# Channel layer: splits and sums on VectorE alone, token sums kept in DRAM, both first products of part one's last groups issued together

## The chip, the cores and the metric

The kernel runs on one core of a Trainium2 chip. The metric is device time in microseconds (us), the median of three runs. TensorE (PE in the profile) multiplies, VectorE (DVE), ScalarE (ACT) and GpSimd (POOL) do the elementwise work, and SyncE (SP) issues the DMAs.

## The reference

Three layers follow each other on 4 sequences of 576 tokens with 512 channels: windowed attention, a low-rank token mix with a channel layer, and a gated spatial layer. The change sits in the channel layer, the two lines with `w_ch1` and `w_ch2`.

```python
x = attention(q, k, v)                          # 8 heads, window of 128, bias by distance
h = x.transpose(0, 2, 1) @ U @ V
u = x + h.transpose(0, 2, 1)
ch = np.maximum(u @ w_ch1, 0.0) @ w_ch2         # 512 -> 2048 -> 512
y = u + ch
h = np.maximum(y @ w_in, 0.0)                   # then gate, spatial mix, w_out
...
```

## The kernel before

Every float32 operand of a large product is split into a high part (rounded to a narrower format on ScalarE) and a low part (operand minus high part, `minus`, L563). A product is then three matmuls: high by high, low weight by high, high weight by low.

The channel layer's 2048 hidden channels are worked off in four parts of 512. **Part 0** uses plain products: six early groups of 256 tokens run beside attention, and two last groups of 384 tokens follow it (`ffn_group`). A group has a first product (`u @ w_ch1`, L513 to L515, 48 matmuls in a group of 384) and a second product (L550 to L552, again 48). **Parts 1 to 3** each have three groups of 768 tokens (`seven_group`), named a, r and c, in the orders a r c, c a r, r a c. A group's first product is done for pairs of blocks with seven products instead of eight (L705 to L707, 84 matmuls), for which sums and differences of blocks of the weights (`pair_forms`) and of the tokens (`token_forms`) are made and split first. Its second product has 96 matmuls. The seven forms are named "11", "2", "1", "3", "12", "22" and "4"; three of them ("11", "12", "4") are plain blocks of u, the other four are sums. A token form holds two k-blocks, each with a high and a low tile of 128 x 384.

When a part starts, its weights are new: w_ch1 blocks are loaded, decoded from their 64-bit form by four VectorE instructions of 512 columns (L416, L417, L420, L423; tile `st`), turned into forms (256 columns each), and the four w_ch2 blocks (`w2s`) are loaded, decoded, rounded on ScalarE (L370) and given their low part on L568 (VectorE) or L569 (GpSimd). The low part of the last w_ch2 block of a part is what the first second-product matmuls of that part's first group need last. After each first product VectorE combines the PSUM results (tile `c`, L712) and takes the low part of the hidden values (tile `hl`, L719); after each second product it adds PSUM into `y` (L750).

Which engine takes a split or a sum is chosen by a planner (`Plan.run`). It lists all tasks with an engine or several, a cost, a priority and their dependencies, and lays them out in time; each engine then executes its list strictly in order. For `ANY = ("POOL", "DVE")` (L572) it takes whichever engine can start. In the plan, an instruction on GpSimd and one on VectorE that both work in SBUF do not overlap (`port=True`); on the chip nothing keeps them apart. Loads go through SyncE's queue, also in the order of the plan. Token forms are single-buffered: 20 slots `xd` and 8 slots `x` hold exactly one set of seven.

Of the kernel before, what the change touches and what calls it, by code (L numbers as in the profile page):

```python
# [74 lines left out]
def f32(ap):  # L75
    return ap.bitcast(F32)
# [31 lines left out]
class Ring:  # L108
# [3 lines left out]
    last = {}  # L112
# [164 lines left out]
def mm(n, m=128):  # L277
    return (max(n, 2 * m) + m / 4) / 2400


def dve(n):
    return n / 960 + 0.066
# [6 lines left out]
def act(n, src=0.06, aps=0):  # L289
    return n / 1200 + src + 0.09 * aps  # L290
# [7 lines left out]
def tile_kernel(ctx, tc, qT, kT, v, U, V, w1, w2, w_in, wspT, bsp, w_out, bias, out):  # L298
# [42 lines left out]
    def in_psum():  # L341
        return psum

    r_wa = Ring(in_left, "wa", 0, more=[f"wa_{i % 12}" for i in range(8, 20)])
    r_w1, r_w2 = (Ring(in_left, "wa", 0, more=[f"wa_{i + j}" for j in range(4)]) for i in (0, 4))
# [149 lines left out]

    def ffn_group(t0, n, wts, prio, first, evac, early):

        hs, ls = split_u(t0, n, evac, early)
        nf = len(wts)
        hid = []  # L500
        for i in range(0, nf, 2 if early else 1):
            per = min(2, nf - i) if early else 1
            if not early:
                turn[0] += 1
            f1 = (r_f1 if early or turn[0] % 4 == 0 else r_at).new([128, per, n], F32)
            for j in range(per):
                wt = wts[i + j][0]

                def f1mm(f1=f1, j=j, wt=wt):
                    for k in range(4):  # L510
                        (a, ia, _), (l, il, _) = hs[k], ls[k]
                        o = f1[:, j]
                        nc.tensor.matmul(o, wt[:, 0, k], a[ia], start=k == 0, stop=False)  # L513
                        nc.tensor.matmul(o, wt[:, 1, k], a[ia], start=False, stop=False)
                        nc.tensor.matmul(o, wt[:, 0, k], l[il], start=False, stop=k == 3)  # L515

                P.add("PE", 12 * mm(n), f1mm, r=[p for x in hs + ls for p in x[2]] + [wt.part(0), wt.part(1)],
                      w=[f1], prio=prio)
            hh, hl = r_h.new([128, per, n], F32R), r_h.new([128, per, n], F32R)
            P.add("ACT", act(per * n), lambda f1=f1, hh=hh: nc.scalar.activation(  # L520
                out=hh.ap(), in_=f1.ap(), func=AF.Relu), r=[f1], w=[hh], prio=evac)
            P.add("DVE", dve(per * n), lambda f1=f1, hh=hh, hl=hl: nc.vector.scalar_tensor_tensor(
                out=hl.ap(), in0=f1.ap(), scalar=0.0, in1=f32(hh.ap()), op0=ALU.max, op1=ALU.subtract),
                r=[f1, hh], w=[hl], prio=evac)
            hid += [(hh, hl, j) for j in range(per)]

            if not early:
                if i == 0:
                    accs = [r.new([128, 1, n], F32) for r in (r_acc, r_sc, r_sc, r_sc)]
                for e in range(4):  # L530
                    second(wts, hid, i, (e,), accs[e], n, prio)
        if early:
            for e in (0, 2):
                acc = r_acc.new([128, 2, n], F32)
                for i in range(nf):
                    second(wts, hid, i, (e, e + 1), acc, n, prio)
                collect(t0, n, (e, e + 1), acc, first, evac)
        else:
            for e in range(4):
                collect(t0, n, (e,), accs[e], first, evac)  # L540

# [29 lines left out]

    ANY = ("POOL", "DVE")  # L572
    FORMS = ("11", "2", "1", "3", "12", "22", "4")
# [55 lines left out]

    def token_forms(which, prio):  # L630

# [9 lines left out]
        for k in range(2):  # L641
# [26 lines left out]
            def plain(name, to=None):  # L668
                hi, lo = res[to or name][k]
                kb, ts = (k, t1) if name == "11" else (k + 2, t1 if name == "12" else t2)  # L670
                for b, s, m, o in ts:
# [4 lines left out]
                          lambda m=m, o=o: f32(hi[:, o : o + m]), r=[ub, hi.part(o)], w=[lo.part(o)], prio=prio)  # L676

            plain("11")
            total("3", (k + 2, 1), (k, 1))
# [7 lines left out]
            split("4", "22")  # L687
            plain("22", "4")
        return res

# [317 lines left out]
    for g in range(NB):  # L1008
        ffn_group(g * 256, 256, parts_w[0], 1e4 + g, True, K["evac"], True)

# [4 lines left out]

    base = 2e4
    for t0 in range(NB * 256, NT, N3):
        ffn_group(t0, N3, parts_w[0], base, True, base - 0.5, False)
        base += 1
    xf, last = None, None  # L1020
    for qi, order in ((1, "arc"), (2, "car"), (3, "rac")):
        forms = [pair_forms(qi, pair, base - K["pf"][pair]) for pair in range(2)]
        w2s = []
        for f in range(4):
            r0 = (sum(PARTS[:qi]) + f) * 128
            w2s.append((None, weights(r_wa, block(w2, r0, r0 + 128, 0, E), 1, E, base - K["p2"] + f / 10, ways=ANY)))
        for which in order:
            if which != last:
                xf, last = token_forms(which, base - K["xf"]), which
            seven_group(which, xf, forms, w2s, base, base - 0.5)  # L1030
            base += 1
# [229 lines left out]

K = dict(parts=(4, 4, 4, 4), flex='xeht', cp=0, wp=0, low=6, w0=7, w0s=0.6, nb=6, evac=40.0, nst=3, d0=7, d0s=0.91, lowd=5, nq=3, pn=1, pf=(1.6, 1.4), p2=1.2, xf=0.7, pi=(1.3, 0.9))

# [39 lines left out]
```

## Time and profile before

| | |
|---|---|
| median of 3 runs | 744.98 us (744.17 to 745.14) |
| the profiled execution | 746.02 us |
| its span, first to last instruction | 744.2 us |
| TensorE busy | 717.3 us, 96% of the span |
| VectorE busy | 535.0 us, 72% |
| ScalarE busy | 339.1 us, 46% |
| GpSimd busy | 189.0 us, 25% |
| mean granted TensorE clock | 0.995 |

The time of an execution is its span and what lies around it (1.8 us here). TensorE's busy share is a modelled one: matmuls are pipelined, and each starts about 0.175 us after the one before (384 columns) while it is shown 0.34 us long. So TensorE is read from the starts and from its idle time, not from busy time. Attention fills about the first 196 us, the last two groups of part 0 the time to 238 us, parts 1 to 3 the time to 531 us, the spatial layer the rest.

### The profile page before, as it was taken

The numbers are of one execution on the slowest core, as the hardware profiler recorded it, in microseconds if no ns is written. First come the engines' busy times: TensorE is split into PE (matmuls) and PEld (weight loads), VectorE is DVE, ScalarE is ACT, GpSimd is POOL, SyncE is SP. The second block draws the span as 40 slices with busy tenths as digits, with TensorE's granted clock in tenths as the row PEclk, the third lists the DMA queues.
The fourth block names the chain that finished last, engine by engine and source line by source line (L and its number), as shares of the span: only waits on it lengthen the run. The fifth ranks groups of instructions, "written<-read, shape, count | busy, mean of one in ns | idle before, by whom it ended". The sixth has DMA issues, their size and how long they took to land.

```text
span 744.2 us, 14920 instructions
## 1 busy us (share of the span) xinstructions
PE 717.3 (96%) x5808; PEld 670.0 (90%) x5808; DVE 535.0 (72%) x1403; ACT 339.1 (46%) x920; POOL 189.0 (25%) x232
## 2 busy tenths in 40 slices
PE   7877999999999999999999998999999999999998
PEld 5656988888999999999999998999999899898896
DVE  5989978685648999598995989978989426326141
ACT  5777757373414724246152462524564333333322
POOL 1243330210622425123231323421335101002000
PEclk9999999999999999999999999999999999999999
DMA  7765313100006000212001230006320100100102
GB/s 226 251 212 145 107 49 99 49 19 2 1 1 196 4 1 1 78 42 108 1 1 29 85 114 1 1 0 199 104 74 1 43 15 1 58 15 1 57 1 71
DMA packets 29164, 45.83 MB, mean 62 GB/s; under 512 B 5029, under 2 KB 18341, under 8 KB 29093
## 3 DMA queue, kind: packets, MB, share of 16 engines
q1 hardware_dynamic: 29092, 44.87, 18.9%
q8 instruction: 46, 0.75, 0.5%
q14 instruction: 26, 0.20, 0.1%
HBM read 39.85 MB, written 4.72 MB: 60 GB/s over the span
## 4 chain that ended last, share of the span: by engine, by line
PE 78%; DVE 13%; issue 4%; DMA 3%; ACT 1%; SPq 1%; POOL 1%; ACTq 0%; POOLq 0%; DVEq 0%
PE sc L552 7%; PE sc L551 7%; PE sc L550 6%; PE at L705 5%; PE at L707 5%; PE at L706 5%; PE sc L1088 3%; PE sc L1090 3%; PE sc L1089 3%; PE at L1090 2%; PE at L1088 2%; PE at L1089 2%; DVE hl L719 2%; PE at L880 2%; PE at L918 2%
## 5 line engine op out<-in xcount | busy, mean ns | idle before, releaser
L551 PE MATMUL sc<-h,wa 128*128 128x384 f32 x312 | 105.6, 339 | 4.5 <-DVE wa L568 4.5
L550 PE MATMUL sc<-h,wa 128*128 128x384 f32 x312 | 105.4, 338 | 0.2 <-ACT wa L370 0.2
L552 PE MATMUL sc<-hl,wa 128*128 128x384 f32 x288 | 98.6, 342 | 0.6 <-DVE hl L719 0.5
L569 POOL TENSOR_TENSOR wa<-st,wa 128x512 fp32r<-128x512 f32 (+2 forms) x44 | 45.9, 1050 | 178.0 <-ACT wa L370 142.7
L850 ACT ACTIVATE p<-p,nmax 128x192 f32<-128x192 f32 (+1 forms) x144 | 61.5, 431 | 10.1 <-DVE nmax L845 10.0
L551 PEld LDWEIGHTS sc<-h,wa 128*128 128x128 f32 x312 | 59.0, 189 | 5.4 <-DVE wa L568 5.4
L712 DVE TENSOR_TENSOR c<-at,c 128x384 f32<-128x384 f32 x90 | 49.7, 552 | 16.5 <-PE at L707 15.8
L705 PE MATMUL at<-xd,wa 128*128 128x384 f32 x180 | 60.9, 338 | 0.0
L706 PE MATMUL at<-xd,wa 128*128 128x384 f32 x180 | 60.8, 338 | 0.0
L707 PE MATMUL at<-xd,wa 128*128 128x384 f32 x180 | 60.8, 338 | 0.0
L550 PEld LDWEIGHTS sc<-h,wa 128*128 128x128 f32 x312 | 59.0, 189 | 0.5 <-ACT wa L370 0.5
L552 PEld LDWEIGHTS sc<-hl,wa 128*128 128x128 f32 x288 | 54.5, 189 | 1.2 <-DVE hl L719 1.2
L750 DVE TENSOR_TENSOR y<-sc,y 128x384 f32<-128x384 f32 (+1 forms) x96 | 40.8, 449 | 15.9 <-PE sc L552 15.6
L370 ACT CAST wa<-st 128x256 fp32r<-128x256 f32 (+1 forms) x70 | 32.6, 491 | 42.6 <-DVE st L423 28.6
L845 DVE CUSTOM_DVE_ANT_0 p<-sc,bias 128x192 f32<-128x192 f32 (+1 forms) x144 | 40.0, 327 | 9.3 <-PE sc L834 9.2
L834 PE MATMUL sc<-kr,qr 64*64 64x192 f32 (+2 forms) x576 | 33.7, 334 | 9.1 <-DMA kr<-in_kT 4.4
L719 DVE SCALAR_TENSOR_TENSOR hl<-c,h 128x384 fp32r<-128x384 f32 x54 | 37.5, 708 | 0.4
L568 DVE TENSOR_TENSOR u<-y,u 128x576 fp32r<-128x576 f32 x9 | 6.6, 753 | 41.8 <-ACT u L1101 41.8
L834 PEld LDWEIGHTS sc<-kr,qr 64*64 64x64 f32 x576 | 22.3, 141 | 14.9 <-issue 5.1
L717 ACT ACTIVATE h<-c 128x384 fp32r<-128x384 f32 x54 | 28.3, 524 | 14.1 <-DVE c L712 13.5
L705 PEld LDWEIGHTS at<-xd,wa 128*128 128x128 f32 x180 | 33.8, 188 | 0.1
L706 PEld LDWEIGHTS at<-xd,wa 128*128 128x128 f32 x180 | 33.8, 188 | 0.0
(350 smaller groups left out, 2154.3 us busy)
## 6 DMA issues: line engine op xcount, KB each, us to landing
wa<-in_w SPq DMA_DIRECT2D x32, 512.0 KB, 4.5
qr<-in_qT SPq DMA_DIRECT2D x16, 288.0 KB, 3.8
kr<-in_kT SPq DMA_DIRECT2D x16, 288.0 KB, 4.2
vr<-in_v SPq DMA_DIRECT2D x16, 256.0 KB, 2.9
wa<-in_w_in SPq DMA_DIRECT2D x8, 512.0 KB, 4.5
out<-h SPq DMA_DIRECT2D x15, 256.0 KB, 2.0
wb<-in_w_out SPq DMA_DIRECT2D x4, 512.0 KB, 4.6
raw<-in_wspT SPq DMA_DIRECT2D x4, 288.0 KB, 2.8
```

Source lines behind the costliest of these rows:

```text
L550: nc.tensor.matmul(o, wt[:, 0, 0, c], hh[:, j], start=i == 0 and x == 0, stop=False, skip_group_check=True)
L551: nc.tensor.matmul(o, wt[:, 1, 0, c], hh[:, j], start=False, stop=False, skip_group_check=True)
L552: nc.tensor.matmul(o, wt[:, 0, 0, c], hl[:, j], start=False, stop=i == len(wts) - 1, skip_group_check=True)
L569: "POOL": (pool_tt(n), lambda: nc.gpsimd.tensor_tensor(out=out(), in0=in0(), in1=in1(), op=op)),
L705: nc.tensor.matmul(o.ap(), wh()[:, k], xh.ap(), start=start and k == 0, stop=False, skip_group_check=True)
L706: nc.tensor.matmul(o.ap(), wl()[:, k], xh.ap(), start=False, stop=False, skip_group_check=True)
L707: nc.tensor.matmul(o.ap(), wh()[:, k], xl.ap(), start=False, stop=k == 1, skip_group_check=True)
L712: P.add("DVE", dve(N3), lambda: nc.vector.tensor_tensor(out=out.ap(), in0=ps_.ap(), in1=sb.ap(), op=ALU.add), r=[ps_, sb], w=[out], prio=0)
L719: P.add("DVE", dve(N3), lambda: nc.vector.scalar_tensor_tensor(out=hl[:, 0], in0=src.ap(), scalar=0.0, in1=f32(hh[:, 0]), op0=ALU.max, op1 ...
L750: P.add("DVE", dve(m), lambda acc=acc, dst=dst, s=s, m=m, o=o: nc.vector.tensor_tensor(out=dst[:, s : s + m], in0=acc[:, 0, o : o + m], in ...
L834: nc.tensor.matmul(s[o : o + 64, c0 : c0 + k1 - k0], qr[d, 64 * t : 64 * t + 64], kr[d, k0:k1], start=True, stop=True, skip_group_check=True)
L850: nc.scalar.activation(out=o(), in_=o(), func=AF.Exp, scale=-1.0, bias=nmax[:, sl, t : t + 1], accum_out=sums[:, sl, t : t + 1])
```

## The change

Four things are changed.

1. `ANY` becomes `("DVE",)`: the low parts, sums and differences of weights and tokens in the channel layer, and the low parts in the spatial layer that used the same name, are made on VectorE alone. Eight low parts of part 0's weights, the low parts of u in part 0 and some of attention's rescaling stay on GpSimd.
2. `token_forms` keeps the four summed forms ("2", "1", "3", "22") of a, r and c in DRAM when it first makes them (16 DMAs of 196 KB for each of the three). When a later part needs them again, they are loaded (16 DMAs) instead of made; the three plain forms are made as before. Of seven calls three store and four load.
3. The two last groups of part 0 issue both first products, then both second products; their PSUM and SBUF buffers come from the rings that the parts behind use (`r_f4`, `r_a4`, `r_hl`).
4. `ffn_group` is split into `early_group` and code in the main loop, with helpers `first_of` and `leave_one`; the early groups issue what they issued.

```diff
+    dram = ctx.enter_context(tc.tile_pool(name="dram", bufs=1, space=bass.MemoryType.DRAM))
...
+    def leave_one(src, n, hh, hl, r, prio):
+
+        P.add("ACT", act(n), lambda: nc.scalar.activation(out=hh.ap(), in_=src(), func=AF.Relu), r=r, w=[hh], prio=prio)
+        P.add("DVE", dve(n), lambda: nc.vector.scalar_tensor_tensor(
+            out=hl.ap(), in0=src(), scalar=0.0, in1=f32(hh.ap()), op0=ALU.max, op1=ALU.subtract), r=r + [hh], w=[hl], prio=prio)
...
-    ANY = ("POOL", "DVE")
+    ANY = K["any"]
...
+            if which in spilled:
+                plain("11")
+                plain("12")
+                plain("22", "4")
+                for name in ("2", "1", "3", "22"):
+                    for i, t in enumerate(res[name][k]):
+                        d = spilled[which][name, k, i]
+                        P.dma(128, N3, lambda t=t, d=d: nc.sync.dma_start(out=f32(t.ap()), in_=f32(d.ap())), r=[d], w=[t],
+                              prio=prio + FORMS.index(name) / 100)
+                continue
             plain("11")
...
+        if spill and which not in spilled:
+            ring = Ring(in_dram, "forms" + which, 16)
+            keep = spilled[which] = {}
+            for name in ("2", "1", "3", "22"):
+                for k in range(2):
+                    for i, t in enumerate(res[name][k]):
+                        d = keep[name, k, i] = ring.new([128, N3], F32R)
+                        P.dma(128, N3, lambda t=t, d=d: nc.sync.dma_start(out=f32(d.ap()), in_=f32(t.ap())), r=[t], w=[d], prio=prio + 0.3)
...
     base = 2e4
+    rest_groups = []
     for t0 in range(NB * 256, NT, N3):
-        ffn_group(t0, N3, parts_w[0], base, True, base - 0.5, False)
+        hs, ls = split_u(t0, N3, base - 0.5, False)
+        hid = []
+        for f in range(4):
+            f1 = r_f4.new([128, 1, N3], F32)
...
+            hh, hl = r_h.new([128, 1, N3], F32R), r_hl.new([128, 1, N3], F32R)
+            leave_one(f1.ap, N3, hh, hl, r=[f1], prio=base - 0.5)
+            hid.append((hh, hl, 0))
+        rest_groups.append((t0, hid))
+    for t0, hid in rest_groups:
+        for e in range(4):
+            acc = r_a4.new([128, 1, N3], F32)
+            for i in range(4):
+                second(parts_w[0], hid, i, (e,), acc, N3, base + 0.1)
+            collect(t0, N3, (e,), acc, True, base - 0.5)
         base += 1
...
-                xf, last = token_forms(which, base - K["xf"]), which
+                xf, last = token_forms(which, base - K["xf"], K["spill"]), which
...
-K = dict(parts=(4, 4, 4, 4), flex='xeht', cp=0, wp=0, low=6, w0=7, w0s=0.6, nb=6, evac=40.0, nst=3, d0=7, d0s=0.91, lowd=5, nq=3, pn=1, pf=(1.6, 1.4), p2=1.2, xf=0.7, pi=(1.3, 0.9))
+K = dict(parts=(4, 4, 4, 4), flex='xeht', cp=0, wp=0, low=6, w0=7, w0s=0.6, nb=6, evac=40.0, nst=3, d0=7, d0s=0.91, lowd=5, nq=3, pn=1, pf=(1.6, 1.4), p2=1.2, xf=0.7, spill=1, any=("DVE",), pi=(1.3, 0.9))
```

In the built programs TensorE has the same number of matmuls of the same shapes. GpSimd has 119 instructions fewer (237 to 118), VectorE 46 more (1405 to 1451), ScalarE 31 fewer (778 to 747), SyncE 112 DMAs more (150 to 262).

VectorE where part 2 begins, around the low part of its last w_ch2 block (`wa_4909<-st_4793`), in the program before. `hl` and `c` are the group's hidden values, `st` a block being decoded:

```order
L420 SCALAR_TENSOR_TENSOR st_4793<-wa_4737,st_4793 128x512
L719 SCALAR_TENSOR_TENSOR hl_4870<-c_4726,h_4782 128x384
L712 TENSOR_TENSOR c_4803<-at_4795,c_4803 128x384
L719 SCALAR_TENSOR_TENSOR hl_4882<-at_4784,h_4854 128x384
L712 TENSOR_TENSOR c_4818<-at_4809,c_4818 128x384
L423 SCALAR_TENSOR_TENSOR st_4793<-wa_4737,st_4793 128x512
L719 SCALAR_TENSOR_TENSOR hl_4904<-c_4753,h_4768 128x384
L719 SCALAR_TENSOR_TENSOR hl_4911<-c_4735,h_4816 128x384
L719 SCALAR_TENSOR_TENSOR hl_4916<-c_4803,h_4887 128x384
L568 TENSOR_TENSOR wa_4909<-st_4793,wa_4909 128x512
```

The same place in the changed program (`wa_4996<-st_4885`):

```order
L560 TENSOR_TENSOR wa_4944<-st_4864,wa_4944 128x512
L724 TENSOR_TENSOR c_4895<-at_4887,c_4895 128x384
L428 SCALAR_TENSOR_TENSOR st_4885<-wa_4829,st_4885 128x512
L724 TENSOR_TENSOR c_4912<-at_4901,c_4912 128x384
L731 SCALAR_TENSOR_TENSOR hl_4998<-c_4815,h_4874 128x384
L731 SCALAR_TENSOR_TENSOR hl_5006<-c_4845,h_4860 128x384
L560 TENSOR_TENSOR wa_4996<-st_4885,wa_4996 128x512
L731 SCALAR_TENSOR_TENSOR hl_5021<-c_4826,h_4908 128x384
```

The last block's decoding now ends ahead of the last PSUM sum (`c_4912`), and two `hl` instead of four instructions stand between that sum and the low part; the low part of the block before it (`wa_4944`), which GpSimd made, stands in the row as well.

SyncE's queue where part 2's weights are loaded, before:

```order
L404 DMA wa_4544<-in_w2 128x1024
L404 DMA wa_4695<-in_w2 128x1024
L404 DMA wa_4717<-in_w2 128x1024
L404 DMA wa_4737<-in_w2 128x1024
L404 DMA wa_4763<-in_w1 128x4x256
L404 DMA wa_5438<-in_w1 128x4x256
L404 DMA wa_5500<-in_w1 128x4x256
```

And in the changed program; `formsa` is the DRAM copy of a's forms:

```order
L409 DMA wa_4783<-in_w2 128x1024
L409 DMA wa_4805<-in_w2 128x1024
L409 DMA wa_4829<-in_w2 128x1024
L409 DMA wa_4855<-in_w1 128x4x256
L679 DMA xd_4910<-formsa_3210 128x384
L679 DMA xd_4919<-formsa_3231 128x384
L679 DMA xd_4930<-formsa_3501 128x384
L679 DMA xd_4940<-formsa_3506 128x384
L679 DMA xd_4953<-formsa_3202 128x384
```

Behind part 2's weights (the last row of these, `wa_4855`, is a block that part 3 will use) the 16 loads of a's forms follow; before, part 3's blocks came next.

## Rows read from the trace of the kernel before

**Rows 1.** Profile page: busy us (share of the span) and instructions of each engine.

```profile
PE 717.3 (96%) x5808; PEld 670.0 (90%) x5808; DVE 535.0 (72%) x1403; ACT 339.1 (46%) x920; POOL 189.0 (25%) x232
```

**Rows 2.** Waits of TensorE: us in total, times, the longest.

```profile
PE sc L551 <- DVE wa L568: 4.5, 3, 2.4
...
PE f L513 <- DVE h L522: 1.1, 2, 0.7
...
PE sc L552 <- DVE hl L719: 0.5, 1, 0.5
...
PE sc L550 <- ACT wa L370: 0.2, 1, 0.2
```

**Rows 3.** Stretches: length, then busy us (instructions) of each engine, granted clock, DMA.

```profile
core 0: us, PE busy (x) PEld busy (x) DVE busy (x) ACT busy (x) POOL busy (x), PEclk, DMA share, GB/s
...
196.00:238.00 42.00, 41.89 (x263) 41.57 (x263) 23.26 (x48) 12.04 (x26) 11.49 (x13) 1.00 0.24 66
238.00:531.00 293.00, 287.76 (x1623) 285.34 (x1623) 256.42 (x521) 122.38 (x277) 85.70 (x82) 0.99 0.14 45
531.00:741.00 210.00, 209.86 (x1277) 191.90 (x1275) 103.15 (x235) 77.34 (x171) 39.46 (x47) 1.00 0.12 38
```

**Rows 4.** TensorE in time where part 3 begins: start, us, [idle before <-releaser].

```profile
449.33 0.33 PE L550 MATMUL sc<-h,wa 128*128 128x384 f32 x1
...
450.39 0.33 PE L550 MATMUL sc<-h,wa 128*128 128x384 f32 x1
453.12 0.69 PE L551 MATMUL sc<-h,wa 128*128 128x384 f32 x1 [2.41 <-DVE wa L568]
453.61 0.52 PE L552 MATMUL sc<-hl,wa 128*128 128x384 f32 x1
...
456.17 0.34 PE L551 MATMUL sc<-h,wa 128*128 128x384 f32 x1
```

**Rows 5.** Five microseconds around that wait, columns as in group 3.

```profile
450.00:455.00 5.00, 2.59 (x11) 2.27 (x10) 5.00 (x8) 0.00 (x0) 2.06 (x2) 0.77 0.00 0
```

**Rows 6.** Chain of work that ended last, there: start, us, what.

```profile
444.40 0.47 DVE c L712
444.87 0.60 DVE st L420
445.47 0.47 DVE hl L719
...
446.90 0.56 DVE c L712
447.46 1.17 DVE st L423
448.62 3.85 DVE hl L719 x3
452.47 0.61 DVE wa L568
```

**Rows 7.** GpSimd in time there: start, us, instruction.

```profile
447.05 2.44 POOL L569 TENSOR_TENSOR xd<-t,xd 128x384 fp32r<-128x384 f32 x2
449.46 1.33 POOL L569 TENSOR_TENSOR x<-u,x 128x384 fp32r<-128x384 f32 x1
450.75 1.31 POOL L569 TENSOR_TENSOR t<-u 128x384 f32<-128x384 f32 x1
```

**Rows 8.** Line 719 on VectorE: ns minimum/median/maximum; `c` lies in SBUF, `at` in PSUM.

```profile
L719 DVE SCALAR_TENSOR_TENSOR hl<-c,h x54: 541/549/1371, 251.4 to 516.7; 128x384 fp32r<-128x384 f32 x54
L719 DVE SCALAR_TENSOR_TENSOR hl<-at,h x18: 542/550/558, 246.6 to 513.0; 128x384 fp32r<-128x384 f32 x18
```

**Rows 9.** SyncE in time before part 3: three loads issued.

```profile
430.05 1.42 SPq L404 DMA_DIRECT2D wa<-in_w  x3
```

**Rows 10.** DMAs from 20 to 40 us: queue traffic, then one issue line (KB each, us to landing).

```profile
q1 hardware_dynamic: 3836, 5.47, 78.4%
...
wa<-in_w SPq DMA_DIRECT2D x6, 512.0 KB, 7.2
```

**Rows 11.** VectorE and GpSimd in time at the end of the second sequence's attention.

```profile
93.65 1.28 DVE L568 TENSOR_TENSOR st<-st 128x256 f32<-128x256 f32 x3
...
94.68 0.84 POOL L569 TENSOR_TENSOR wa<-st,wa 128x256 fp32r<-128x256 f32 x1 [3.54 <-ACT wa L370]
94.84 0.69 DVE L522 SCALAR_TENSOR_TENSOR h<-f,h 128x512 fp32r<-128x512 f32 x1
```

**Rows 12.** Profile page: issue line of the output's stores, KB each, us to landing.

```profile
out<-h SPq DMA_DIRECT2D x15, 256.0 KB, 2.0
```

More of the change, by code (lines that the diff above doesn't have):

```diff
@@ L342, in in_psum, with in_dram @@
         return psum
+    dram = ctx.enter_context(tc.tile_pool(name="dram", bufs=1, space=bass.MemoryType.DRAM))
+    def in_dram():
+        return dram
     r_wa = Ring(in_left, "wa", 0, more=[f"wa_{i % 12}" for i in range(8, 20)])
@@ L494, in split_u @@
         return hs, ls
-    def ffn_group(t0, n, wts, prio, first, evac, early):
-        hs, ls = split_u(t0, n, evac, early)
-        nf = len(wts)
-        hid = []
[L501 to L506, printed above, removed]
-                wt = wts[i + j][0]
[L509 to L540, printed above, removed]
@@ new lines, in first_of @@
+    def first_of(o, wt, hs, ls):
+        for k in range(4):
+            (a, ia, _), (l, il, _) = hs[k], ls[k]
+            nc.tensor.matmul(o, wt[:, 0, k], a[ia], start=k == 0, stop=False)
+            nc.tensor.matmul(o, wt[:, 1, k], a[ia], start=False, stop=False)
+            nc.tensor.matmul(o, wt[:, 0, k], l[il], start=False, stop=k == 3)
+    def leave_one(src, n, hh, hl, r, prio):
+        P.add("ACT", act(n), lambda: nc.scalar.activation(out=hh.ap(), in_=src(), func=AF.Relu), r=r, w=[hh], prio=prio)
+        P.add("DVE", dve(n), lambda: nc.vector.scalar_tensor_tensor(
+            out=hl.ap(), in0=src(), scalar=0.0, in1=f32(hh.ap()), op0=ALU.max, op1=ALU.subtract), r=r + [hh], w=[hl], prio=prio)
@@ new lines, in early_group @@
+    def early_group(t0, n, wts, prio, evac):
+        hs, ls = split_u(t0, n, evac, True)
+        hid = []
+        for i in range(0, 4, 2):
+            f1 = r_f1.new([128, 2, n], F32)
+            for j in range(2):
+                wt = wts[i + j][0]
+                P.add("PE", 12 * mm(n), lambda f1=f1, j=j, wt=wt: first_of(f1[:, j], wt, hs, ls),
+                      r=[p for x in hs + ls for p in x[2]] + [wt.part(0), wt.part(1)], w=[f1], prio=prio)
+            hh, hl = r_h.new([128, 2, n], F32R), r_h.new([128, 2, n], F32R)
+            leave_one(f1.ap, 2 * n, hh, hl, r=[f1], prio=evac)
+            hid += [(hh, hl, j) for j in range(2)]
+        for e in (0, 2):
+            acc = r_acc.new([128, 2, n], F32)
+            for i in range(4):
+                second(wts, hid, i, (e, e + 1), acc, n, prio)
+            collect(t0, n, (e, e + 1), acc, True, evac)
@@ L628, in tile_kernel, with token_forms @@
     N3 = 384
-    def token_forms(which, prio):
+    spilled = {}
+    def token_forms(which, prio, spill):
         res = {}
@@ L1008, in tile_kernel @@
     for g in range(NB):
-        ffn_group(g * 256, 256, parts_w[0], 1e4 + g, True, K["evac"], True)
+        early_group(g * 256, 256, parts_w[0], 1e4 + g, K["evac"])
     r_xd, r_hl, r_c, r_t = (Ring(in_chan, tag, n, [end_att]) for tag, n in (("xd", 20), ("hl", 8), ("c", 6), ("t", 3)))
@@ L1016, in tile_kernel @@
     base = 2e4
+    rest_groups = []
     for t0 in range(NB * 256, NT, N3):
-        ffn_group(t0, N3, parts_w[0], base, True, base - 0.5, False)
+        hs, ls = split_u(t0, N3, base - 0.5, False)
+        hid = []
+        for f in range(4):
+            f1 = r_f4.new([128, 1, N3], F32)
+            P.add("PE", 12 * mm(N3), lambda f1=f1, wt=parts_w[0][f][0], hs=hs, ls=ls: first_of(f1[:, 0], wt, hs, ls),
+                  r=[p for x in hs + ls for p in x[2]] + [parts_w[0][f][0].part(0), parts_w[0][f][0].part(1)], w=[f1], prio=base)
+            hh, hl = r_h.new([128, 1, N3], F32R), r_hl.new([128, 1, N3], F32R)
[5 more added lines that the diff above has]
+            acc = r_a4.new([128, 1, N3], F32)
+            for i in range(4):
+                second(parts_w[0], hid, i, (e,), acc, N3, base + 0.1)
+            collect(t0, N3, (e,), acc, True, base - 0.5)
         base += 1
```

## The prediction

> **What bounds the kernel now.** I read the engines' totals first [rows 1], then who makes TensorE wait [rows 2], then the stages [rows 3], and last, instruction by instruction, the longest of the waits [rows 4 to 7]. TensorE is busy for 717.3 of the 744.2 us of the span. The stages show where the missing time is: 18 us before 196 us, in attention, which the change hardly touches; 0.1 us in part 0's last two groups; 5.2 us in parts 1 to 3; 0.1 us in the spatial layer. The matmuls stay the same in number and shape, so the change can win only what TensorE loses to waits. In parts 1 to 3 these are 4.5 us in three waits for a low part of w_ch2, made by VectorE on L568, 0.5 us for an `hl`, and 0.2 us for a high part [rows 2].
>
> The longest is that at 453 us [rows 4]. It costs more than its 2.41 us. Ahead of it, seven matmuls start within 1.06 us, 0.177 us apart, though each is shown 0.33 us long; the next was therefore due at 450.57 and started at 453.12, 2.55 us late. Idle time understates each gap by about 0.15 us. Behind the wait ten starts (453.12 to 456.17, nine distances) take 3.05 us where 1.59 are usual, another 1.46 us. The granted clock of those five microseconds is 0.77 [rows 5]: after TensorE stood still the chip granted the lower of its two levels (1.2 instead of 2.4 GHz) for a while. So the pool is 5.2 + 5 x 0.15 + 1.5 = **7.4 us**.
>
> Why VectorE was late is in the chain [rows 6]. Behind the last PSUM sum (446.90) it decodes 512 columns in 1.17 us, the same form that takes 0.60 us at 444.87; then three `hl` in 3.85 us, a form that takes 0.47 at 445.47; then the low part in 0.61. At the clean prices that is 0.47 + 0.60 + 3 x 0.47 + 0.61 = 3.1 us from 446.90, so ready at 450.0, and TensorE wanted it at 450.57. It would not have waited. GpSimd works from 447.05 to 452.06 without a break [rows 7]. Over the run `hl` takes 541 ns at best and 549 in the median but up to 1371 when its input `c` lies in SBUF, and never over 558 when it lies in PSUM [rows 8]. So a VectorE instruction with both inputs in SBUF is held up while GpSimd works; here 5.0 us of GpSimd's work held VectorE for 0.57 + 2.44 = 3.0 us.
>
> **The change part by part.**
>
> *Splits and sums on VectorE.* The longest wait and its 1.5 us of slow clock vanish if nothing runs on GpSimd at that time, and in the order of the changed program nothing does once part 0's token splits are done. In exchange VectorE takes over work. Counted in the order: 13 more low parts of 512 columns, 26 forms of 256, 9 of 576, and 17 small ones, at 0.60 us for 512 and 0.47 for 384 [rows 6], the others by columns between (256 about 0.33, 576 about 0.67, the small ones about 0.25): 8 + 9 + 6 + 4 = 27 us. The loads from DRAM take off 18 token instructions of 384 or 192 columns net, 8 us. So VectorE gets 19 us more, and gets back what it now loses beside GpSimd: between nothing and 0.6 of the 85.7 us that GpSimd is busy from 238 to 531 us [rows 3], by the ratio 3.0 to 5.0 above; nearest to the true value is the upper end, since most of GpSimd's instructions there stand beside two-input work. VectorE's 256 us in that stage should therefore end between 224 and 275.
>
> A busy total does not decide; the tight places do. At the start of each part the order gives: VectorE has 14.4 us of work (9 instructions of 512 columns at 0.60, six at about 0.33, 13 of 384 at 0.47, three of 256) from the start of the first product to the low part of the last w_ch2 block; four of them wait for the last PSUM sum, which comes after 87 matmuls, 15.3 us. The two `hl` and the low part behind that sum are done some 2.2 us later; the first matmul that reads this low part stands 25 places on, 4.4 us, and the tightest `hl` 23 to 26 places on, with 0.8 us to spare. So no wait, unless VectorE is more than 0.8 us behind. That covers all three w_ch2 waits and the one for the high part: 4.5 + 0.2 + 4 x 0.15 + 1.5 = 6.8 us.
>
> The second tight place is new. In part 1 nothing can be loaded yet, and the forms for r are in pieces of 192. From the end of the first first product to the end of the next, 177 matmuls or 31.2 us, VectorE has 52 instructions of 384 columns, 22 of 192, 3 of 512 and 2 decodings: 32.5 us. It ends up 1.3 us behind, but the first form that it makes late ("2" of r) is finished about 14.2 us into a stretch in which it is wanted at 17.9. I take nothing for it, and up to 3 us for the range.
>
> *Forms kept in DRAM.* 64 loads and 48 stores of 196 KB. Stores hold a slot until they have read it, which is well before its next writer. For the loads: the slots of form "2" come free after 54 of a group's 84 first matmuls, and the next group reads them 30 + 96 + 6 = 132 matmuls or 23.2 us later. SyncE issues a load in about 0.47 us [rows 9], 16 in 7.6 us. The queue moved 5.47 MB in 20 us [rows 10], so 3.15 MB need 11.5 us. Hidden, cost nothing; ScalarE is freed of 32 casts besides. SyncE's queue behind them: the next part's blocks, whose slots come free later anyway.
>
> *Both first products ahead.* TensorE loses only 0.1 us there now [rows 3]. What it moves is when part 0's w_ch1 slots are free: 96 instead of 24 matmuls ahead of part 1's first product by the order, 12.7 us earlier, so pair two of part 1's forms is not squeezed against the group's start. Nothing by itself; without it the first of the three waits could stay.
>
> *Attention.* Four forms of 256 columns go from GpSimd to VectorE just ahead of an `h` for which TensorE waits 0.7 us [rows 2, 11]. One more beside what is held up now: +0.7 to -0.7 us, taken as 0.
>
> Sum: 6.8 us for the four waits; the `hl` wait (0.5 + 0.15 us) I leave standing, as the price of one tight place that slips. The profiled execution would go from 746.02 to about 739.2 us, its span to 737.4. That execution lies 1.0 us above the median; taken off the median, 744.98 - 6.8 = **738.2 us**.
>
> **A rule that speaks against it.** The trace shows VectorE busy for 256 of 293 us in parts 1 to 3 [rows 3]. The Trainium skill, "Perfetto Trace Analysis", section "Optimizing Scalar/DVE Operations", says that work may be moved off a saturated VectorE, even to GpSimd, and adds that between these two it might not help, as they share a port. By its first half the change would go the wrong way and the first rival would win; by its second half the forecast. The Trainium skill, "SBUF — State Buffer", section "Who interferes with whom", calls that port an exclusive lock; the trace agrees ([rows 8], 1371 against 549 ns).
>
> **The rivals.**
>
> *VectorE becomes the bound, part of the gain is given back.* If its instructions, with their waits for ScalarE's high parts, come 10% slower than the clean rows, it loses 1.2 us ahead of each part's last sum and has 0.8 in hand: 0.4 us late three times, with 0.15 us a gap 1.7 us in all, 739.9; at 15% 3 x (1.9 - 0.8 + 0.15) = 3.8 us, 742.0; at 20% 743.5. r's forms would even then come at 17.0 of 17.9 us. For it: 32.5 us of work in 31.2, and all low parts now in one queue. Against: the clean rows already hold VectorE's own overhead, and up to 51 us of contention go.
>
> *The loads from DRAM come late: slower than before.* If transfers follow each other at the 2.0 us that a store of 256 KB takes to land [rows 12], 16 last 32 us, and the last four (form "22") are wanted 30 + 96 + 30 = 156 matmuls or 27.5 us after the first can start: 4.5 us late, four times, 18 us, so 756. It decides from 1.72 us a load. Against: the six 512 KB loads, 7.2 us to landing each, overlapped in a queue that moved 5.47 MB in 20 us [rows 10]. The Trainium skill, "DMA: Bandwidth & Descriptors", section "Anatomy of one DMA", gives, for GpSimd's queue, about 2.0 us fixed for each DMA and 436 GB/s. An estimate from it is 2.45 us a load, 39 us for 16 one behind the other; no run here shows such a row of small loads.
>
> *It does not do what it says.* The low part still stands behind the last PSUM sum; if VectorE is held up by something else than GpSimd (ScalarE, DMA traffic, now more of it), the waits stay: 744.5 to 745.5.
>
> **How the numbers follow.** Forecast (736.3 to 740) 0.70; VectorE the bound (740 to 743.5) 0.14; no effect 0.07; slower 0.09. The likeliest is 738.2. The range: below, the whole 7.4, the 0.7 in attention and half a microsecond of spread, 736.3; above, the first rival up to 742, leaving out about 2 in 10. A difference of 0.2%, 1.5 us, is about what three runs can tell from none. Faster 0.83, same 0.08, slower 0.09.
>
> **What would show it.** In the changed profile: TensorE's waits between 238 and 531 us below 1.5 us in sum, none over 1 us, no stretch there with a granted clock below 0.95; `hl` from `c` never over 0.6 us; GpSimd idle there; VectorE 224 to 275 us, nearer the lower end; no wait of TensorE for a DMA of `xd` or `x`. Wrong, if TensorE waits for `xd` or `x` loaded from DRAM, or again for L568's low part at a part's start while GpSimd is idle, or if the spatial layer, where VectorE also takes over, shows waits that it has not now.

## The result and the profile after

The changed kernel took **739.7 us** against 744.98, a ratio of 0.9914 (95% interval 0.9887 to 0.9941); beside the first experiments it took 736.73 against 746.08, 0.9886 (0.9864 to 0.9908). The gain is 6.4 to 8.5 us, 738.2 was predicted. One of its first five executions, 1167.51 us at a granted clock of 0.56, counts in the median of 739.7 but not in the ratio (the other four have a median of 738.9), and the profile below is that of an execution of 737.27 us, span 735.4.

Busy time and instructions of each engine, after (as [rows 1]):

```profile
PE 713.5 (97%) x5808; PEld 668.8 (91%) x5808; DVE 516.6 (70%) x1449; ACT 324.9 (44%) x889; POOL 66.4 (9%) x113
```

The three stretches after, columns as in [rows 3]; parts 1 to 3 now end at 522 us instead of 531:

```profile
196.00:238.00 42.00, 42.00 (x265) 42.00 (x264) 30.06 (x71) 14.27 (x31) 4.23 (x5) 1.00 0.35 105
238.00:522.00 284.00, 284.00 (x1620) 284.00 (x1619) 228.57 (x510) 105.66 (x238) 0.00 (x0) 1.00 0.35 117
522.00:732.00 210.00, 210.00 (x1279) 192.14 (x1277) 106.15 (x263) 77.66 (x173) 15.11 (x22) 1.00 0.11 38
```

TensorE has no idle time left in parts 1 to 3, at a granted clock of 1.00; GpSimd does nothing there. TensorE waits neither for the low part (made on what is now L560, read on L543) nor for `hl` (L731). `hl` after (as [rows 8]) no longer takes over 0.56 us, and the loads from DRAM land in 3.8 us (issue line: KB of 1024 bytes each, median us to landing), twelve of them issued in 5.55 us (SyncE in time):

```profile
L731 DVE SCALAR_TENSOR_TENSOR hl<-c,h x54: 545/550/560, 254.0 to 507.8; 128x384 fp32r<-128x384 f32 x54
```

```profile
xd<-formsa SPq DMA_DIRECT2D x24, 192.0 KB, 3.8
```

```profile
341.68 5.55 SPq L679 DMA_DIRECT2D xd<-formsa  x12
```

From the start of part 1's first matmul to that of the spatial layer's first one, read from TensorE in time, before took 530.94 - 238.16 = 292.78 us and after 522.20 - 237.97 = 284.23. These 8.55 us are the whole difference of the two spans (8.8) but for 0.25. In what follows "parts 1 to 3" is this length, and times go with the ratio to the kernel before, run beside it.

### The profile page after: what moved, and what is told of

It reads as the page before. It is cut to its first block, busy times and chain, and to the rows that moved or that the text cites. A ratio compares the mean times of both kernels' runs of the same rounds, so it can differ in the third digit from the quotient of the medians.

```text
span 1165.6 us, 14977 instructions
## 1 busy us (share of the span) xinstructions
PE 1150.5 (99%) x5808; PEld 886.8 (76%) x5808; DVE 531.6 (46%) x1449; ACT 329.2 (28%) x889; POOL 65.1 (6%) x113
## 4 chain that ended last, share of the span: by engine, by line
PE 98%; DVE 1%; ACT 0%; DMA 0%; issue 0%; SPq 0%; ACTq 0%
PE sc L544 8%; PE sc L543 8%; PE sc L542 8%; PE at L717 6%; PE at L719 6%; PE at L718 6%; PE at L930 4%; PE sc L846 3%; PE at L892 3%; PE sc L1118 3%; PE sc L1117 3%; PE sc L1116 3%; PE at L1117 3%; PE at L1116 3%; PE at L1118 3%; PE f L505 2%
## 5 line engine op out<-in xcount | busy, mean ns | idle before, releaser
L544 PE MATMUL sc<-hl,wa 128*128 128x384 f32 x320 | 153.6, 480 | 0.0
L542 PE MATMUL sc<-h,wa 128*128 128x384 f32 x320 | 153.6, 480 | 0.0
L543 PE MATMUL sc<-h,wa 128*128 128x384 f32 x320 | 153.4, 479 | 0.0
L543 PEld LDWEIGHTS sc<-h,wa 128*128 128x128 f32 x320 | 69.6, 218 | 22.7 <-issue 0.8
L544 PEld LDWEIGHTS sc<-hl,wa 128*128 128x128 f32 x320 | 69.5, 217 | 22.8 <-issue 1.1
L542 PEld LDWEIGHTS sc<-h,wa 128*128 128x128 f32 x320 | 69.4, 217 | 22.6 <-issue 1.1
L719 PE MATMUL at<-xd,wa 128*128 128x384 f32 x180 | 86.4, 480 | 0.0
L718 PE MATMUL at<-xd,wa 128*128 128x384 f32 x180 | 86.3, 479 | 0.0
L717 PE MATMUL at<-xd,wa 128*128 128x384 f32 x180 | 86.2, 479 | 0.0
L846 PE MATMUL sc<-kr,qr 64*64 64x192 f32 (+2 forms) x576 | 50.0, 444 | 8.2 <-DMA kr<-in_kT 4.6
L717 PEld LDWEIGHTS at<-xd,wa 128*128 128x128 f32 x180 | 39.1, 217 | 12.9 <-issue 0.8
L718 PEld LDWEIGHTS at<-xd,wa 128*128 128x128 f32 x180 | 39.2, 218 | 12.7 <-issue 0.5
L719 PEld LDWEIGHTS at<-xd,wa 128*128 128x128 f32 x180 | 39.0, 217 | 12.6 <-issue 0.3
L930 PEld LDWEIGHTS at<-ph,vr 64*64 64x64 f32 (+1 forms) x1024 | 39.9, 184 | 10.5 <-ACT ph L375 4.2
L930 PE MATMUL at<-ph,vr 64*64 64x64 f32 (+1 forms) x1024 | 44.3, 276 | 2.3 <-ACT ph L375 2.3
L892 PE MATMUL at<-ident,p 128*128 128x128 f32 x208 | 45.8, 390 | 0.5 <-ACT p L862 0.5
L560 DVE TENSOR_TENSOR u<-y,u 128x576 fp32r<-128x576 f32 x16 | 11.9, 752 | 73.1 <-ACT u L1129 73.0
```

Source lines behind the costliest of these rows:

```text
L542: nc.tensor.matmul(o, wt[:, 0, 0, c], hh[:, j], start=i == 0 and x == 0, stop=False, skip_group_check=True)
L543: nc.tensor.matmul(o, wt[:, 1, 0, c], hh[:, j], start=False, stop=False, skip_group_check=True)
L544: nc.tensor.matmul(o, wt[:, 0, 0, c], hl[:, j], start=False, stop=i == len(wts) - 1, skip_group_check=True)
L717: nc.tensor.matmul(o.ap(), wh()[:, k], xh.ap(), start=start and k == 0, stop=False, skip_group_check=True)
L718: nc.tensor.matmul(o.ap(), wl()[:, k], xh.ap(), start=False, stop=False, skip_group_check=True)
L719: nc.tensor.matmul(o.ap(), wh()[:, k], xl.ap(), start=False, stop=k == 1, skip_group_check=True)
```

## The experiments

**Theory**: the gain comes from VectorE no longer being held up by GpSimd. **Rivals**: it comes from fewer token instructions (DRAM), or from the earlier w_ch1 slots (both first products ahead). The eight on and off combinations of the three edits, "V" all on VectorE, "D" forms in DRAM, "F" both first products ahead (us):

| edits | time | ratio, 95% interval | parts 1 to 3 |
|---|---|---|---|
| none | 744.98 to 746.97 | 1 | 292.78 |
| V | 744.15 | 0.9977 (0.9962 to 0.9993) | 290.72 |
| D | 746.63 | 0.9992 (0.9977 to 1.0006) | 291.19 |
| F | 746.59 | 1.0010 (0.9995 to 1.0024) | 292.05 |
| D F | 742.69 | 0.9961 (0.9942 to 0.9979) | 288.20 |
| V D | 746.14 | 1.0002 (0.9984 to 1.0019) | 291.81 |
| V F | 737.46 | 0.9889 (0.9867 to 0.9912) | 284.23 |
| V D F | 736.73 | 0.9886 (0.9864 to 0.9908) | 284.23 |

### All three (the changed kernel again)

> The changed kernel as it stands, for a profile that can be set beside that of before. Contention theory (GpSimd's work held up VectorE's two-input instructions, and these made TensorE wait): in parts 1 to 3, 238 to about 524 us, TensorE's waits sum to under 1.5 us, none over 1 us; no 10 us window there has a granted clock below 0.95; `hl` from SBUF never over 0.6 us; VectorE busy 224 to 275 us; time 738 to 740. Rival 'VectorE the bound': the waits for L560 low parts or `hl` of 0.5 to 1.3 us at each part's start, sum 2 to 4 us. Rival 'loads late': TensorE waits for `xd` or `x` on a DMA.

All of the first theory's numbers held but the time: 736.73 lies 1.3 us below the 738 to 740 that were expected. Neither rival's waits are there.

### D and F, GpSimd let in again

One entry of the table of settings `K`:

```diff
-any=("DVE",)
+any=("POOL", "DVE")
```

> The changed kernel with GpSimd let in again beside VectorE for splits and sums (one word of the table of settings), forms in DRAM and both first products ahead kept. Contention theory: GpSimd is busy some 60 to 85 us between 238 and 530, `hl` from SBUF reaches over 1 us again, and some 3 to 7 us of the gain go: 741 to 745. Rival 'fewer token instructions' and rival 'earlier w_ch1 slots' (the other two parts of the change make the gain): as fast as the changed kernel, 738 to 740.

742.69: 6.0 us of the gain are gone. Three waits for a low part are back, and `hl` from SBUF takes up to 1376 ns again (GpSimd is busy for 58.12 us from 238 to 522 us):

```profile
PE sc L543 <- DVE wa L560: 3.2, 3, 1.6
```

### V and F, forms made again

```diff
-spill=1
+spill=0
```

> The changed kernel with the summed forms made again for each of the seven calls instead of kept in DRAM; all splits and sums stay on VectorE. Contention theory: VectorE gets 8 us more (4 calls; 18 instructions of about 0.47 net of what is loaded) and ScalarE 32 casts, no wait comes back for GpSimd's sake; time within 1.5 us of the changed kernel, 738 to 741. Rival 'VectorE the bound': the tight places of parts 2 and 3 have now 0.8 us less than nothing, and 1 to 2 us a part are lost: 742 to 745. Rival 'fewer token instructions make the gain': 743 to 745.

737.46, not to be told from the changed kernel. VectorE is busy for 256.11 of 284 us and ScalarE for 120.79, and still TensorE never waits:

```profile
238.00:522.00 284.00, 284.00 (x1620) 283.82 (x1619) 256.11 (x584) 120.79 (x274) 0.00 (x0) 1.00 0.15 50
```

So DRAM forms are worth nothing once GpSimd is out, though they take 74 instructions and 27.5 us from VectorE, where I had expected 18 and 8; the rival "fewer token instructions" falls, and "VectorE the bound" too, at 90% busy.

### V alone

```diff
-    ANY = ("POOL", "DVE")
+    ANY = ("DVE",)
```

> The kernel before with one edit: splits and sums all on VectorE; forms made again in each call, last two groups of part 0 one after the other. Contention theory: the `hl` and low-part waits of parts 2 and 3 go (about 4 to 6 of the 6.8 us), the first one, of part 1, may stay since w_ch1's slots come free late: 739 to 742. Rivals 'fewer token instructions' and 'earlier w_ch1 slots': no gain or a loss, since VectorE only has more to do: 744 to 750.

744.15, a miss: only 1.7 us of 8.5 by the ratio. Parts 2 and 3 run without a wait, as the theory has it, but a new wait stands at part 1's first products. TensorE in time there:

```profile
249.02 0.45 PE L707 MATMUL at<-x,wa 128*128 128x384 f32 x1 [0.41 <-DVE x L568]
252.43 0.69 PE L705 MATMUL at<-xd,wa 128*128 128x384 f32 x1 [2.96 <-DVE hl L719]
252.92 0.52 PE L706 MATMUL at<-xd,wa 128*128 128x384 f32 x1
253.24 0.52 PE L707 MATMUL at<-xd,wa 128*128 128x384 f32 x1
```

and 8 us stretches (columns as in [rows 3]), first of this kernel, then of the changed one:

```profile
238.00:246.00 8.00, 8.00 (x47) 8.00 (x47) 8.00 (x21) 5.51 (x15) 0.00 (x0) 1.00 0.36 114
246.00:254.00 8.00, 4.62 (x21) 3.91 (x20) 7.92 (x16) 6.01 (x14) 0.00 (x0) 0.82 0.00 0
254.00:262.00 8.00, 8.00 (x37) 8.00 (x36) 5.69 (x12) 2.55 (x6) 0.00 (x0) 0.75 0.01 2
```

```profile
238.00:246.00 8.00, 8.00 (x47) 8.00 (x46) 4.72 (x10) 3.53 (x7) 0.00 (x0) 1.00 0.68 256
246.00:254.00 8.00, 8.00 (x48) 8.00 (x47) 8.00 (x17) 7.58 (x22) 0.00 (x0) 1.00 0.21 76
254.00:262.00 8.00, 8.00 (x47) 8.00 (x46) 8.00 (x20) 1.52 (x5) 0.00 (x0) 1.00 0.13 49
```

VectorE works from 238 us on without a break, since w_ch1's second pair is still to be decoded and split then, and the `hl` stands behind that; after the wait matmuls start 0.32 us apart instead of 0.175, at the lower clock. In the changed kernel VectorE has 3.3 us to spare from 238 to 246 us, since it did this work before: it is busy for 30.06 us from 196 to 238 us, not 23.26 [rows 3].

### F alone

The changed kernel with two settings put back:

```diff
-spill=1, any=("DVE",)
+spill=0, any=("POOL", "DVE")
```

> Only the third part of the change: both first products ahead at part 0's end; GpSimd beside VectorE as before, forms made again in each call. If DRAM forms are worth nothing beside GpSimd either: as the run with GpSimd let in again, 742 to 743.5. If they are worth something where VectorE is held up (they take 18 token instructions from VectorE and GpSimd): 744 to 746. The prediction's 'nothing by itself' would be 745 to 746.

746.59, "nothing by itself", as predicted: the waits for low parts (5.6 us, three) and for `hl` (0.5) stay. Against D and F together, DRAM forms are worth 0.0049 of the time, 3.7 us, where GpSimd holds VectorE up.

### V and D, old order in part 0's end

```diff
+            if f == 0:
+                accs = [r_a4.new([128, 1, N3], F32) for _ in range(4)]
+            for e in range(4):
+                second(parts_w[0], hid, f, (e,), accs[e], N3, base)
-        rest_groups.append((t0, hid))
-    for t0, hid in rest_groups:
...
```

> The changed kernel with part 0's last two groups one after the other again (first product of a block, then its second, group after group); all on VectorE, forms in DRAM. Theory now: TensorE waits at part 1's first products for an `hl`, 2 to 4 us and 1 to 2 us of slow clock behind it, since VectorE can start on w_ch1's second pair only after both groups, and has 16 us of work in a row by then; 742 to 745, parts 2 and 3 without waits. Rival (the waits of the kernel before with only VectorE come from forms made again, not from the order): 737 to 739.

746.14: without the third edit nothing of the gain is left, more than I expected. Beside V alone (0.9977) the DRAM forms gave nothing here either. The wait is at part 1's first products, for a token form and an `hl`:

```profile
PE at L719 <- DVE x L560: 4.9, 1, 4.9
PE at L717 <- DVE hl L731: 0.4, 1, 0.4
```

### New order, later preparation

```diff
-            P.dma(rows.stop - rows.start, src.shape[-2] * src.shape[-1], load, w=[part], prio=prio if early is None else early)
+            P.dma(rows.stop - rows.start, src.shape[-2] * src.shape[-1], load, r=hold, w=[part], prio=prio if early is None else early)
...
-            single(st[i], [(0, block(w1, 0, E, c0, c0 + 128, 4))], 4, 128, prio + i / 10, r_wa)
+            single(st[i], [(0, block(w1, 0, E, c0, c0 + 128, 4))], 4, 128, prio + i / 10, r_wa, hold=[y[3][1]] if qi == 1 and pair else ())
```

> The changed kernel, its matmuls at part 0's end in the new order, but the loads of part 1's second w_ch1 pair and first w_ch2 block held until the last group's sum of its second 128 columns is in SBUF, about when the old order gave these slots free (some 234 us instead of 221). Theory 'early slots': VectorE is at work without a break from 238 to 254 us again, and a wait of 2 to 4 us at part 1's first products returns: 741 to 745. Rival 'the order of the matmuls itself' (hidden activations made earlier, sums later): no wait, 736.5 to 738.5.

747.33, above the 741 to 745 that were expected. The edit did less to the loads than I meant: the dependency binds the plan's order and not the transfer, so the three loads are issued from 221.67 us on, not at 234 (in the changed kernel: two from 214.99, one at 221.31; attention ended 1.9 us later here). But the order that comes of it puts the second pair's decoding behind the last sums, as the old order did. VectorE then waits 9.8 us, seven times, for these sums, and TensorE waits five times in part 1's first group, 5.3 us in all; the first two rows of it:

```profile
DVE y L552 <- PE sc L544: 9.8, 7, 1.6
```

```profile
PE at L718 <- DVE wa L560: 1.8, 1, 1.8
PE at L717 <- ACT wa L375: 1.6, 1, 1.6
```

VectorE is busy for 21.74 us from 196 to 238 us here, for 30.06 in the changed kernel. So the matmul order at part 0's end alone is worth nothing; what counts, as far as this run shows it, is that VectorE prepares part 1's second pair before 238 us. A run that held back these loads and left VectorE's sums in place was not made.

### Extra work on GpSimd that reads SBUF

```diff
+            if pair:
+                for _ in range(30):
+                    P.add("POOL", 0.0, lambda hl=o11[1]: nc.gpsimd.tensor_tensor(
+                        out=extra.ap(), in0=f32(hl[:, 0, :96]), in1=f32(hl[:, 0, 96:192]), op=ALU.subtract), r=[o11[1]], w=[extra], prio=0)
...
+    extra = Ring(in_chan, "extra", 1, [end_att]).new([128, 96], F32)
```

> The changed kernel with work on GpSimd that nobody reads: in each of the nine groups of parts 1 to 3, 30 subtractions of 96 columns with both inputs in SBUF, from the second pair's first `hl` on. The order on all other engines is that of the changed kernel, instruction for instruction. Contention theory: GpSimd is busy 70 to 120 us in parts 1 to 3, `hl` from SBUF reaches over 0.8 us, VectorE's busy time there grows by 20 to 60 us, and TensorE's waits for `hl` or low parts return: 739 to 745. Rival 'what made VectorE late was the order and the queueing of its work, not GpSimd's use of SBUF': `hl` stays under 0.6 us and the time at 736 to 738.

745.54, though VectorE and ScalarE execute the changed kernel's list, instruction for instruction. GpSimd is busy for 141 us from 238 to 522 us, more than I expected, and TensorE waits 5.5 us in six waits. The largest, 3.9 us in three, is for `c`, which stands in VectorE's list behind slowed work; only once did VectorE wait for GpSimd itself (0.8 us). `hl` reaches 750 ns, not the 800 that were expected: these subtractions are shorter than the old ones. VectorE's forms from 238 to 522 us (busy us, mean ns), changed kernel and then this one:

```profile
L724 DVE TENSOR_TENSOR c<-at,c 128x384 f32<-128x384 f32 x90 | 49.9, 554 | 21.8 <-PE at L719 21.2
L731 DVE SCALAR_TENSOR_TENSOR hl<-c,h 128x384 fp32r<-128x384 f32 x54 | 28.9, 550 | 0.3 <-ACT h L729 0.2
L425 DVE SCALAR_TENSOR_TENSOR st<-wa,st 128x512 uint32<-128x512 uint32 x26 | 17.6, 684 | 0.1
L422 DVE TENSOR_SCALAR st<-st 128x512 uint32<-128x512 uint32 x26 | 10.6, 420 | 0.1
```

```profile
L724 DVE TENSOR_TENSOR c<-at,c 128x384 f32<-128x384 f32 x90 | 49.6, 552 | 20.9 <-PE at L719 20.5
L731 DVE SCALAR_TENSOR_TENSOR hl<-c,h 128x384 fp32r<-128x384 f32 x54 | 32.6, 618 | 0.3 <-ACT h L729 0.2
L425 DVE SCALAR_TENSOR_TENSOR st<-wa,st 128x512 uint32<-128x512 uint32 x24 | 18.1, 759 | 0.1
L422 DVE TENSOR_SCALAR st<-st 128x512 uint32<-128x512 uint32 x24 | 11.7, 495 | 0.1
```

The form with an operand in PSUM (`c`) is unchanged; the three that work in SBUF alone take 11 to 18% longer, the one with a single input (L422) too. This settles the theory: GpSimd's work alone, with no change of any order, makes TensorE wait again, if for other tiles than before.

### Extra fills on GpSimd

In place of the subtractions:

```diff
+                for _ in range(80):
+                    P.add("POOL", 0.0, lambda hl=o11[1]: nc.gpsimd.memset(extra.ap(), 0.0), r=[o11[1]], w=[extra], prio=0)
```

> The changed kernel with work on GpSimd that nobody reads, as in the run with extra subtractions, but it only writes: 80 fills of 96 columns in each of the nine groups. The order on the other engines is unchanged. If it is GpSimd's reading of SBUF that holds VectorE up: forms of VectorE with all operands in SBUF keep their means (550 ns for `hl` of 384, 684 for a decoding with two inputs), time 736 to 738. If any GpSimd work at all does it: the means rise by a tenth to a fifth again and the time is 740 to 746.

734.03, 0.9843 (0.9818 to 0.9869). GpSimd is busy for 109 us there, `hl` keeps its 550 ns, L425 its 682, and only the single-input forms rise a little (L422 from 420 to 439):

```profile
L748 POOL MEMSET extra<- 128x96 f32 x587 | 109.2, 186 | 33.8
L731 DVE SCALAR_TENSOR_TENSOR hl<-c,h 128x384 fp32r<-128x384 f32 x54 | 28.9, 550 | 0.3 <-ACT h L729 0.2
L422 DVE TENSOR_SCALAR st<-st 128x512 uint32<-128x512 uint32 x27 | 11.5, 439 | 0.1
```

Nearly all fills ran ahead of their place, from 205 to 381 us; still 29 of the 54 `hl` from SBUF overlap one, as 30 of 54 overlap a subtraction in the run before. VectorE's order differs from the changed kernel's only behind 522 us. So it is work of GpSimd that reads SBUF, not work that only writes. The Trainium skill, "SBUF — State Buffer", section "Who interferes with whom", says this: a VectorE instruction with two SBUF inputs contends with a GpSimd one that reads SBUF, not with one that only writes; the trace agrees (618 ns beside subtractions, 550 beside fills). That this kernel beats the changed one I had not expected; the last experiment asks why.

### Part 0's low parts on VectorE too

```diff
-                    nc.gpsimd.tensor_tensor(
+                    nc.vector.tensor_tensor(
...
-    def weights(ring, src, k, c, prio, early=None, on_pool=(False, False), ways=("POOL",)):
+    def weights(ring, src, k, c, prio, early=None, on_pool=(False, False), ways=("DVE",)):
```

> The changed kernel with part 0's low parts too (weights and tokens, 8 + 44 instructions, 38 us of GpSimd's time) moved from GpSimd to VectorE. Contention theory carried on to attention: VectorE gets some 22 us of work before 210 us and gets back less than that, since there GpSimd is busy 47 of 195 us; the one wait for a low part by GpSimd (1.0 us) goes; 735 to 738. Rival, VectorE is the bound in attention's first 90 us (17 to 19 of 20 us busy): 738 to 742.

739.54, 0.9910 (0.9891 to 0.9930): no gain over the changed kernel, so the 735 to 738 of the contention theory is missed, and the time lies in the rival's range. That it is slower than the changed kernel is not clear of noise: the intervals overlap (0.9864 to 0.9908), and in the first result the changed kernel had 0.9914. Attention's first 90 us have VectorE busy for 78.35 us (75.31 in the changed kernel), and TensorE has new waits, for attention's `p` and for a low part that VectorE now makes:

```profile
PE at L892 <- DVE p L884: 2.6, 1, 2.6
...
PE f L507 <- DVE x L492: 1.4, 1, 1.4
```

But other waits shrink, and TensorE's waits before 205 us sum to 16.7 us, to 18.1 in the changed kernel's profile. Part 0's last two groups start at 197.15 us; in the changed kernel and the three runs with extra work or an extra tile, which have the same attention, they start at 194.75 to 197.62. So the profile does not show the rival's loss, and what decides here stays open.

### D alone

The V and D kernel with one setting put back:

```diff
-any=("DVE",)
+any=("POOL", "DVE")
```

> Only the second part of the change: forms kept in DRAM; GpSimd beside VectorE, old order in part 0's end. The forms take some 27 us from VectorE and GpSimd in parts 2 and 3 and nothing in part 1, whose start is the crowded place: the waits of part 1 stay (2 to 4 us with slow clock), those of parts 2 and 3 shrink; 743 to 745.5. If the forms are worth nothing by themselves: 745.5 to 747.

746.63, no gain; my 743 to 745.5 missed it. Beside GpSimd and without the early slots, 4.7 us of waits stay in parts 1 to 3.

### One tile more, nothing else

```diff
+            if pair and not extra.users:
+                P.add("POOL", 0.0, lambda: nc.gpsimd.memset(extra.ap(), 0.0), r=[o11[1]], w=[extra], prio=0)
...
+    extra = Ring(in_chan, "extra", 1, [end_att]).new([128, 96], F32)
```

> The changed kernel with one tile of 96 columns (384 bytes a partition) more in the pool of the channel layer, filled once by GpSimd; nothing else differs, and the order of all engines but for that fill is that of the changed kernel. It moves `xd`, `hl`, `c` and `t` by 384 bytes. In the two runs with extra GpSimd work, which had this tile too, a matmul that reads `xd`, and the step from `hl` to the next block, took 0.173 to 0.175 us from start to start instead of 0.176 to 0.179. If the place of the tiles does that: 93 second products last 16.1 us instead of 16.3, parts 1 to 3 280.5 to 281.5 us instead of 284.2, and the time is 732.5 to 735. If GpSimd's fills do it: 16.3 us, and 736 to 738.

**733.69, 0.9827 (0.9808 to 0.9846)**: the fastest of all, ahead of both kernels. Parts 1 to 3 take 281.13 us. TensorE never idles in either kernel from 238 to 518 us, at a granted clock of 1.00, but it starts 1598 matmuls in the changed kernel and 1615 in this one (PE busy and count, clock, DMA), 175.2 and 173.4 ns each:

```profile
238.00:518.00 280.00, 280.00 (x1598) 1.00 0.35 119
```

```profile
238.00:518.00 280.00, 280.00 (x1615) 1.00 0.35 117
```

VectorE and ScalarE have the changed kernel's order, and GpSimd one short fill more. So the place of the tiles does it, not GpSimd's work. The run with subtractions had this tile too, so its right neighbour is this kernel: the extra reads cost 291.61 - 281.13 = 10.5 us in parts 1 to 3, the extra fills 281.43 - 281.13 = 0.3.

## Why the prediction was right, and where it was not

*The pool.* I put what TensorE lost in parts 1 to 3 at 7.4 us; the changed kernel is 8.55 us shorter there. The mis-sized term is "0.15 us a gap": a gap costs that much more than its wait, but the step behind it is late too, and some late steps are shown without any wait. Before, TensorE in time:

```profile
353.20 0.33 PE L550 MATMUL sc<-h,wa 128*128 128x384 f32 x1
355.14 0.44 PE L551 MATMUL sc<-h,wa 128*128 128x384 f32 x1 [1.61 <-DVE wa L568]
355.42 0.34 PE L552 MATMUL sc<-hl,wa 128*128 128x384 f32 x1
...
385.27 0.34 PE L551 MATMUL sc<-h,wa 128*128 128x384 f32 x1
385.71 0.44 PE L552 MATMUL sc<-hl,wa 128*128 128x384 f32 x1
```

The second row starts 1.94 - 0.175 = 1.77 us late at a wait of 1.61, the next one another 0.1; at 385.71 0.27 us are lost and no wait is shown. Adding up what every step over 0.21 us between two starts of 384 columns has beyond 0.175 gives 8.4.

*The cause*, GpSimd holding up VectorE: right, and shown by the two runs with extra work, reading and only writing, set beside the run with the extra tile. That it takes two SBUF inputs was too narrow (L422 has one).

*The four waits, 6.8 us*: gone. *The `hl` wait, left standing at 0.65*: gone too, so this reserve was wrong by its whole size.

*VectorE's sum.* 224 to 275 us, "nearer the lower end": 228.57. But the terms were off against each other. I gave the stage 19 us more work; the whole kernel has 46 instructions more (1403 to 1449, 47 were counted), but the stage 11 fewer (521 to 510): the work went to the time before 238 us and to the spatial layer. And the contention given back was not up to 51 us: of the 27.9 us that VectorE fell, 11 instructions at 0.45 us make 5, the other 23 are by this estimate contention, 0.27 of GpSimd's 85.70 us and not 0.6 (the ratio was read at one place alone). `hl` from SBUF alone gives 8.5 of them, 54 times 708 - 550 ns. Before, same columns:

```profile
L719 DVE SCALAR_TENSOR_TENSOR hl<-c,h 128x384 fp32r<-128x384 f32 x54 | 37.5, 708 | 0.4
```

*The tight stretch in part 1, costs nothing*: right, with both first products ahead. *DRAM loads hidden*: right; landings of 3.8 us overlap, and the rival's row of loads one behind the other did not come. *Attention 0*: no change is seen; part 0's last two groups start at 195.67 us, before at 195.64, but single executions of the same attention differ by up to 2.9 us there, so a change of half a microsecond would not show. *Spatial layer*: no new wait.

*Both first products ahead: "nothing by itself; without it the first of the three waits could stay".* The first half is right (F alone). The second was far too small, and this is the step that failed: without it the whole gain goes (V and D). I had counted VectorE's 14.4 us at a part's start in the order of the changed program, where part 1's second pair is prepared already, and never counted what stands there when it is not. The sum came out right because it took all edits together; that it put the whole gain down to one edit, which alone gives 1.7 us, and still met the time was luck.

*The rule that spoke against it* (the Trainium skill, "Perfetto Trace Analysis", section "Optimizing Scalar/DVE Operations"). In parts 1 to 3 VectorE was busy for 256.42 of 293 us [rows 3], 88%. With GpSimd's work taken over and no forms in DRAM (V and F) it did 63 instructions more in 256.11 us of 284, and TensorE never waited: the second half of the rule, the shared port, won. In attention's first 90 us the same move took it from 75.31 to 78.35 us and gained nothing; no run here shows clearly that it lost, so there the rule stays open.

## What to carry to other kernels

Taking a helper engine off a shared resource paid here only where the engine left alone had room at the tightest place. So look at that place with the other edits undone, and try edits in pairs: here two of them gave 8.3 us together, and 1.7 us and nothing alone. A busy share does not tell whether an engine is the bound: VectorE 90% busy cost nothing where its work at part 1's start was done ahead (V and F), and 81% busy (V and D, 234.96 of 291 us) cost the whole gain where it was not.

## What the runs showed of the hardware

Where tiles lie in SBUF changed TensorE's pace by 1% with no list changed but for GpSimd's one fill: with one more tile of 384 bytes a partition beside `xd`, `hl`, `c` and `t`, a matmul of 384 columns starts after 173.4 instead of 175.2 ns. The mean busy time of matmuls that read the moved `hl` and `xd` falls, that of those that read the unmoved `x` does not (each time the changed kernel, then that with the extra tile):

```profile
L544 PE MATMUL sc<-hl,wa 128*128 128x384 f32 x288 | 97.9, 340 | 0.0
L717 PE MATMUL at<-xd,wa 128*128 128x384 f32 x180 | 60.8, 338 | 0.0
L717 PE MATMUL at<-x,wa 128*128 128x384 f32 x72 | 24.1, 334 | 0.0
```

```profile
L544 PE MATMUL sc<-hl,wa 128*128 128x384 f32 x288 | 96.2, 334 | 0.0
L717 PE MATMUL at<-xd,wa 128*128 128x384 f32 x178 | 59.6, 335 | 0.0
L717 PE MATMUL at<-x,wa 128*128 128x384 f32 x72 | 24.1, 335 | 0.0
```

Those that read `h` fall as well, from 336 to 334 ns. Which property of the place decides was not tried. It has no part in the gain itself: from the start of an `hl` matmul to the next start it is 178.3 to 178.5 ns on average (steps up to 0.21 us) in the kernel before, the changed one and every run without the tile, and 173.1 to 173.5 in the three runs with it.

Attention alone moves by 2.9 us from one execution to the next: part 0's last two groups start at 194.75 to 197.62 us in the changed kernel and the three runs with extra work or an extra tile. In the run with later preparation, where they start at 197.56, the granted clock was 0.70 from 60 to 70 us; it was 1.00 in the changed kernel's profile (195.67). So lengths of a stage, not spans of single profiles, were compared here.
